# A fused attention, feed-forward and soft-MoE kernel: other column parts at the end, low sums in PSUM, halves before the selector, and a new written order

## The chip, the cores and the metric

The kernel runs on one core of a Trainium2 chip. The time is device microseconds (us) of one launch, measured on the chip; a figure for a kernel is the median of its runs.

## What is computed

Three stages, all in f32 outside (shapes: q, k, v 2 x 8 x 768 x 64; x 1536 x 512; w1 8 x 512 x 1024; w2 8 x 1024 x 512):

```python
# 1. clustered attention, 16 head-batches, 16 centroids per head
q_assign = argmax(einsum('bhsd,hcd->bhsc', q_n, c_n), -1)      # the same for k
scores = where(q_assign == k_assign, q @ k.T / sqrt(D), -1e9)
x = softmax(scores) @ v                                         # -> [1536, 512]
# 2. feed-forward with h * relu6(h + 3) / 6
x = act(x @ w_in) @ w_out                                       # 512 -> 2048 -> 512
# 3. soft MoE: 8 experts with 4 slots each
logits = x @ phi                                                # [1536, 32]
slot_input = softmax(logits, 0).T @ x                           # [32, 512]
slot_out[e] = relu(slot_input[e] @ w1[e]) @ w2[e]
out = softmax(logits, 1) @ slot_out                             # [1536, 512]
```

## The kernel before

The whole program is one function of some 1,170 small generators, most of them a few instructions long between two `yield`s. `ev` (L270) collects them; `flush` (L273) runs them in an order that is written out by hand: the string `ORDER` lists, step by step, the number of the generator that issues its next piece. Each engine works through its instructions in the order in which they were issued, and so does each queue of DMA issues (SP's for loads and half of the stores, ScalarE's for the other half). A second string, `ROOMS`, says which buffer of a pool each named tile gets; a tile's first write waits for the last reader of what stood in that buffer.

**Attention.** A head-batch `i` (called a head below) has queries and keys split into f16 high and low halves and transposed (`qk1t`). `as_mm` (L461) multiplies the twelve 128-row tiles of q and k with the centroids `ct`, which are themselves two f16 halves side by side: a matmul gives 2 x 16 columns, the sums with the centroids' high halves and those with their low halves. ScalarE copies the low columns to a tile `ac`, VectorE adds them to the high ones; then `as_mm` and `as_max` (L486) find the largest of 16 with its index and write a one-hot tile, `as_put` (L504) puts it beside q and k as mask columns, and it is transposed too: for head 0 by TensorE, for the others by a DMA (`qk2t`). `maxq` and `maxr` take the rows' maxima, `shift` (L572) writes them into `qk2t` as one more row, and `scores` (L587) makes the masked scores of which ScalarE takes the exponential. `keep` (L374) issues filler matmuls into a PSUM tile `kw` that nobody reads.

**End.** The slots' input (`slot_in`, `slot_t` L1290) goes through `layer1` (L1409; four experts side by side in 32-column strips, two groups `g`), `relu`, `turn` (transposes) and `layer2` (L1446; group 0) to the slot outputs. Group 1's layer 2 is done in two column parts, `PARTS` (L1017): columns 0 to 383 and then 384 to 511, so that output columns of part 0 leave while part 1 is still computed. `fetch` (L1041) loads the weights over SP's queue, two DMAs of 512 KB for a 1 MB tile `wk_n` (`rooms`, L1023, names the buffer: four of them are the tiles `pr_0` to `pr_3`). The chunks of kind "d" are group 1's second-layer weights `w2[e]`, 1,024 rows as 8 chunks `c` of 128, of which the first half of the tiles (hf 0) takes chunks 1 to 4 of part 0's columns and the whole of chunk 0, the second (hf 1) the rest of part 0, and after all of part 0 the rest of part 1.

`layer2_part` (L1465) computes a part of group 1 and copies it from PSUM to SBUF in f32 (`o2s`). In `o2s` the 32 slots x 4 experts stand as 128 rows of which only each expert's own four slots count. `selectors` (L1340) builds an f32 matrix that picks these rows, three times over; `slots_out` (L1355) multiplies it with `o2s` of both groups (96 rows: three copies of the slots' outputs), ScalarE scales the 96 rows into f16 (`s16`), and VectorE overwrites the last 32 with the rest, the low half. `combine` (L1374) multiplies the combining weights (transposed `cT`) with `s16`, scales, and stores: batch 0 over ScalarE's queue, batch 1 over SP's, in part 0 three stores for each batch, in part 1 one.

## Time and profile before

| | us |
|---|---|
| median of 3 runs (lowest, highest) | 450.44 (450.15, 451.37) |
| the profiled execution: its own time | 451.0 |
| its span | 449.1 |

| engine | busy us | share of the span |
|---|---|---|
| TensorE (PE) | 429.5 | 96% |
| its weight loads (PEld) | 276.1 | 61% |
| ScalarE (ACT) | 309.8 | 69% |
| VectorE (DVE) | 274.9 | 61% |
| GpSimd (POOL) | 251.1 | 56% |

The mean granted clock of TensorE is 0.991 of full speed. The span goes from the first to the last instruction of the profile; the execution's own time is 1.9 us longer. Busy time counts instructions on an engine, not register, semaphore or DMA-issuing ones; the weight loads run beside matmuls. A share of the span is an average over stages of a different kind, so that views by stretch, waits, and the chain of work that ended last are needed beside it.

### The profile page before, as it was taken

The page shows a single profiled execution, that of the slowest core. Times are in us where ns is not written, and L with a number is a line of the kernel's source. Part 1 is how long each engine was busy: PE and PEld are TensorE (multiplying, and loading weights), DVE is VectorE, ACT ScalarE, POOL GpSimd, SP SyncE. Part 2 cuts the span into 40 slices and gives each one's busy share as a digit, 9 for nine tenths or more (in the row PEclk, how much of TensorE's full clock was granted, in tenths as well). Part 3 has the DMA queues.
Part 4 walks back from the last instruction along what each step waited for, and adds up shares of the span by engine and source line. Part 5 has one row for each costly group of instructions (what it writes and reads, how often), then busy time and mean ns, then how long its engine had stood idle before and what let it go on. Part 6 is the DMA issues. An engine that isn't in the chain of part 4 may idle for free.

```text
span 449.1 us, 11732 instructions
## 1 busy us (share of the span) xinstructions
PE 429.5 (96%) x4866; PEld 276.1 (61%) x4866; DVE 274.9 (61%) x479; ACT 309.8 (69%) x508; POOL 251.1 (56%) x229
## 2 busy tenths in 40 slices
PE   8899999999999999999999999999999999889983
PEld 6567778777886556565656567774555445623432
DVE  5989999999866686484666577513434225540322
ACT  7789999988999887888778789874344344501112
POOL 6557588965665676678759788884232333130000
PEclk9999999999999999999999999999999999989997
DMA  8999958997677998407664719907996888799978
GB/s 268 250 201 221 262 89 230 232 234 257 223 173 108 273 260 190 140 14 153 131 165 86 175 22 341 227 14 143 290 393 183 200 216 273 249 378 347 382 211 278
DMA packets 126645, 95.23 MB, mean 212 GB/s; under 512 B 95360, under 2 KB 111744, under 8 KB 126592
## 3 DMA queue, kind: packets, MB, share of 16 engines
q1 hardware_dynamic: 122672, 88.69, 75.1%
q10 hardware_dynamic: 3920, 5.80, 3.6%
q8 instruction: 38, 0.62, 0.6%
q14 instruction: 15, 0.12, 0.1%
HBM read 64.06 MB, written 7.34 MB: 159 GB/s over the span
## 4 chain that ended last, share of the span: by engine, by line
PE 73%; DVE 11%; DMA 6%; ACT 5%; issue 2%; POOL 1%; SPq 0%; DVEq 0%; ACTq 0%; POOLq 0%
PE h L745 27%; PE st L591 5%; PE sm L553 5%; PE st L595 5%; DVE mxs L569 4%; PE acc L661 4%; PE acc L674 3%; DMA wk<-in_moe_w_dram 2%; PE acc L667 2%; PE acc L666 2%; DMA pr<-in_moe_w_dram 2%; PE z L853 2%; PE kw L377 2%; PE lg L796 2%; DMA qk1t<-pr 1%
## 5 line engine op out<-in xcount | busy, mean ns | idle before, releaser
L368 POOL TENSOR_TENSOR pp<-p,pp 128x768 f16<-128x768 f32 x72 | 118.4, 1653 | 46.6 <-ACT pp L358 31.7
L745 PE MATMUL h<-wq,xt 128*128 128x512 f16 x576 | 134.1, 379 | 0.0
L569 DVE TENSOR_REDUCE mxs<-sm 128x1 f32<-128x768 f32 x96 | 89.1, 951 | 20.7 <-PE sm L553 19.9
L745 PEld LDWEIGHTS <-xt 128*128 128x128 f16 x576 | 54.4, 98 | 59.4 <-issue 2.1
L368 POOL TENSOR_TENSOR ghl<-r,ghl 128x1024 f16<-128x1024 f32 (+1 forms) x25 | 50.3, 2014 | 59.1 <-ACT ghl L358 54.6
L639 ACT ACTIVATE p<-st 128x768 f32<-128x768 f32 x72 | 58.2, 811 | 18.3 <-PE st L595 14.4
L358 ACT ACTIVATE pp<-p 128x768 f16<-128x768 f32 x72 | 60.4, 842 | 2.8 <-PE acc L674 1.8
L764 DVE SCALAR_TENSOR_TENSOR r<-r,h 128x1024 f32<-128x1024 f32 (+1 forms) x26 | 29.5, 1137 | 28.6 <-ACT r L762 28.3
L762 ACT ACTIVATE r<-h,b_relu 128x1024 f32<-128x1024 f32 (+1 forms) x26 | 27.1, 1047 | 17.6 <-POOL ghl L368 9.4
L591 PE MATMUL st<-qk1t 128*128 128x384 f16 x144 | 35.1, 325 | 2.3 <-DVE qk2t L578 0.7
L358 ACT ACTIVATE ghl<-r 128x1024 f16<-128x1024 f32 (+1 forms) x26 | 25.5, 986 | 16.1 <-PE z L853 8.4
L667 PE MATMUL acc<-v,pp 128*128 128x64 f16 x432 | 36.1, 194 | 0.0
L666 PE MATMUL acc<-v,pp 128*128 128x65 f16 x432 | 36.1, 192 | 0.0
L661 PE MATMUL acc<-v,pp 128*128 128x65 f32 x288 | 35.6, 273 | 0.0
L661 PEld LDWEIGHTS acc<-v,pp 128*128 128x128 f32 x288 | 34.7, 192 | 0.9
L595 PE MATMUL st<-qk2t 102*128 102x384 f16 x144 | 35.2, 325 | 0.0
L553 PE MATMUL sm<-qk2t 80*128 80x384 f16 x144 | 34.4, 325 | 0.7 <-ACT wot L989 0.2
L666 PEld LDWEIGHTS <-pp 128*128 128x128 f16 x432 | 31.5, 99 | 2.9
L368 POOL TENSOR_TENSOR pr<-pr,pr 128x768 f16<-128x768 f32 x15 | 25.2, 1677 | 13.6 <-ACT pr L358 10.3
L667 PEld LDWEIGHTS <-pp 128*128 128x128 f16 x432 | 29.2, 96 | 2.8
L358 ACT ACTIVATE pr<-pr 128x768 f32<-128x768 f32 (+2 forms) x32 | 26.3, 823 | 4.0 <-DMA qk1t<-pr 2.2
L377 PE MATMUL kw<-ident,ident 128*128 128x256 f16 x136 | 22.9, 294 | 2.6 <-POOL b_relu L870 1.7
(223 smaller groups left out, 801.7 us busy)
## 6 DMA issues: line engine op xcount, KB each, us to landing
wk<-in_moe_w_dram SPq DMA_DIRECT2D x36, 512.0 KB, 6.7
wi<-in_moe_w_in_dram SPq DMA_DIRECT2D x16, 512.0 KB, 6.2
wod<-in_moe_w_out_dram SPq DMA_DIRECT2D x16, 512.0 KB, 4.8
pr<-in_moe_w_dram SPq DMA_DIRECT2D x12, 512.0 KB, 6.5
wos<-wo ACTq DMA_DIRECT2D x8, 512.0 KB, 3.3
wk<-wos SPq DMA_DIRECT2D x8, 512.0 KB, 5.1
pr<-in_q_dram SPq DMA_DIRECT2D x16, 192.0 KB, 4.4
pr<-in_k_dram SPq DMA_DIRECT2D x16, 192.0 KB, 4.3
```

The source lines that it names most:

```text
L358: nc.scalar.activation(out, in_, AF.Copy, scale=scale)
L368: (nc.vector if e == "v" else nc.gpsimd).tensor_tensor(out=out, in0=in_, in1=hi, op=ALU.subtract)
L377: nc.tensor.matmul(t[:, 0, 0:256], ident16, ident.bitcast(F16), start=True, stop=True)
L553: nc.tensor.matmul(s[:, j, 0:384], d["qk2t"][0:80, n, 0], d["qk2t"][0:80, 3 * j : 3 * j + 3, 1], start=True, stop=True,)
L569: nc.vector.tensor_reduce(out=mxs[i % 2][:, 96 + n : 97 + n], in_=s[:, :, 0:384], op=ALU.max, axis=AX.XY)
L591: nc.tensor.matmul(s[:, j, 0:384], d["qk1t"][:, t, 1], d["qk1t"][:, 3 * j : 3 * j + 3, 0], start=True, stop=False)
L595: nc.tensor.matmul(s[:, j, 0:384], d["qk2t"][0 : 96 + NT, t, 1], d["qk2t"][0 : 96 + NT, 3 * j : 3 * j + 3, 0], start=False, stop=True,)
L639: nc.scalar.activation(p32, s[:, :, 0:384], AF.Exp, scale=sc_exp)
L661: nc.tensor.matmul(o, p32[:, j, r * P : (r + 1) * P], d["v32"][:, t], start=(t == 0 and n == 0), stop=False)
L666: nc.tensor.matmul(o, hi, v1[:, t, 0:65], start=(t == 0 and n == 0), stop=False)
L667: nc.tensor.matmul(o[:, 0:64], hi, v1[:, t, 65:129], start=False, stop=False)
L745: nc.tensor.matmul(s[:, fb % 2], xt[:, lhs], wq[fb][:, hl, kk], start=(n == 0), stop=(n == 11))
```

## The change

It has five parts.

1. In `as_mm`, for heads 0 and 1 only, the low centroid sums are added in PSUM: 24 matmuls of 16 columns, two for each tile into the same columns, in place of 12 of 32 columns. The copy by ScalarE and the add by VectorE go.
2. `PARTS` becomes 352 and 160 columns. The loads of the "d" chunks are cut otherwise: for part 0 pairs of chunks (2 x 352 columns, 16 loads, before 8 of 4 or 3 chunks and 4 of chunk 0 whole); then for part 1 four chunks of 160 columns in a load (8 loads, as before).
3. The experts' results go to f16 before the selector: `o2_halves` has ScalarE write the high half, scaled by a mask column that is 2^10 on the group's own rows and 0 elsewhere, and VectorE the low half. The mask is built by VectorE (four reductions of 32 x 2 and a scale). The selector is one f16 matrix for both groups; `slots_out` now issues four f16 matmuls, two for 64 rows (high half, twice) and two for 32 rows (low half), and ScalarE and VectorE each copy their rows to `s16`.
4. `layer2_part` yields after every second chunk, so that its matmuls can be issued in four pieces.
5. `ORDER` and `ROOMS` are new throughout.

```diff
 ORDER = (
-    "0 837 807 9 811 8 9 809 0 15 15 803 829 840 0 0 0 16 16 16 16 16 5 10 8 11 13 13 842 848 834 820 8 8 16 16 8 "
+    "9 9 8 15 13 15 16 16 0 13 0 0 1131 840 838 810 822 808 832 7 828 8 12 16 16 8 842 16 818 11 16 16 8 827 8 836 "
...
@@ -463,21 +463,29 @@
         d = st[i]
         pm = psm(f"as_{i}")
         a2 = pm[:, 0 : 24 * C].rearrange("p (n l c) -> p n l c", l=2, c=C)
+        a = a2[:, :, 0]
         for n in range(2 * NT):
-            nc.tensor.matmul(
-                a2[:, n],
-                d["qk1t"][:, n // 2, n % 2],
-                ct[:, :, h * C : (h + 1) * C],
-                start=(n == 0),
-                stop=(n == 2 * NT - 1),
-            )
-        yield
-        a = a2[:, :, 0]
-        ac = sm.tile([P, 12, C], F32, tag="ac", name=f"ac_{i}", bufs=1)
-        nc.scalar.copy(ac, a2[:, :, 1])
-        yield
-        nc.vector.tensor_tensor(out=a, in0=a, in1=ac, op=ALU.add)
-        yield
+            x = d["qk1t"][:, n // 2, n % 2]
+            if i < 2:
+                for l in range(2):
+                    nc.tensor.matmul(
+                        a[:, n],
+                        x,
+                        ct[:, l, h * C : (h + 1) * C],
+                        start=(n == 0 and l == 0),
+                        stop=(n == 2 * NT - 1 and l == 1),
+                    )
+            else:
+                nc.tensor.matmul(
+                    a2[:, n], x, ct[:, :, h * C : (h + 1) * C], start=(n == 0), stop=(n == 2 * NT - 1)
+                )
+        yield
+        if i >= 2:
+            ac = sm.tile([P, 12, C], F32, tag="ac", name=f"ac_{i}", bufs=1)
+            nc.scalar.copy(ac, a2[:, :, 1])
+            yield
+            nc.vector.tensor_tensor(out=a, in0=a, in1=ac, op=ALU.add)
+            yield
         mx = sm.tile([P, 12], F32, tag="mx", name=f"mx_{i}", bufs=2)
         nc.vector.tensor_reduce(out=mx, in_=a, op=ALU.max, axis=AX.X)
         nc.vector.tensor_tensor(out=a, in0=a, in1=mx.unsqueeze(2).to_broadcast([P, 12, C]), op=ALU.is_equal)
@@ -1014,7 +1022,7 @@
 
 
     NG = E // 4
-    PARTS = [(0, 384), (384, 128)]
+    PARTS = [(0, 352), (352, 160)]
     chunks = [("o", c, 0) for c in range(4)]
     chunks += [("1", 4 * g + j, hf) for g in range(NG) for hf in range(2) for j in range(4)]
     chunks += [("2", 4 * g + j, hf) for g in range(NG - 1) for hf in range(2) for j in range(4)]
@@ -1042,40 +1050,22 @@
         n = ring["n"]
         ring["n"] += 1
         kind, e, hf = chunks[n]
-        if kind == "d" and hf == 1:
-
+        if kind == "d":
             ts = []
-            for j in range(4):
+            for j in range(4 if hf else 1):
                 t = room(n + j, rooms[n + j], 2048, f"wk_{n + j}")
-                u = t[:, 0:1152].rearrange("p (c d) -> p c d", c=3)
-                v = t[:, 1152:2048].rearrange("p (c d) -> p c d", c=7)
-                for c in range(1, 8):
-                    wd[e + j, 1, c] = v[:, c - 1]
-                for c in range(5, 8):
-                    wd[e + j, 0, c] = u[:, c - 5]
-                ts.append((u, v))
-            for j in range(4):
+                for p, (c0, w) in enumerate(PARTS):
+                    u = wd[e + j, p, hf] = t[:, 4 * c0 : 4 * c0 + 4 * w].rearrange("p (c d) -> p c d", c=4)
+                    for c in range(4):
+                        wd[e + j, p, 4 * hf + c, "w"] = u[:, c]
+            todo = [(0, hf, r, 2, j) for r in (0, 2) for j in range(4 if hf else 1)]
+            if hf:
+                todo += [(1, f, 0, 4, j) for f in range(2) for j in range(4)]
+            for p, f, r, m, j in todo:
+                c0, w = PARTS[p]
                 src = w2[e + j].rearrange("(p c) d -> p c d", c=8)
-                nc.sync.dma_start(ts[j][0], src[:, 5:8, 0:384])
+                nc.sync.dma_start(wd[e + j, p, f][:, r : r + m], src[:, 4 * f + r : 4 * f + r + m, c0 : c0 + w])
                 yield
-            for lo, hi in ((1, 4), (4, 8)):
-                for j in range(4):
-                    src = w2[e + j].rearrange("(p c) d -> p c d", c=8)
-                    nc.sync.dma_start(ts[j][1][:, lo - 1 : hi - 1], src[:, lo:hi, 384:512])
-                    yield
-            return
-        if kind == "d":
-            src = w2[e].rearrange("(p c) d -> p c d", c=8)
-            t = room(n, rooms[n], 2048, f"wk_{n}")
-            u = t[:, 512:2048].rearrange("p (c d) -> p c d", c=4)
-            wd[e, 0, 0] = t[:, 0:384]
-            wd[e, 1, 0] = t[:, 384:512]
-            for c in range(1, 5):
-                wd[e, 0, c] = u[:, c - 1]
-            nc.sync.dma_start(u, src[:, 1:5, 0:384])
-            yield
-            nc.sync.dma_start(t[:, 0:512], src[:, 0])
-            yield
             return
         if kind == "1":
             src = w1[e].rearrange("(p k) f -> p k f", k=4)[:, 2 * hf : 2 * hf + 2]
@@ -1338,38 +1328,42 @@
         nc.vector.tensor_copy(cT, tp)
 
     def selectors():
-        sel = sl["sel"] = lt2k("a1", 0, [NG, 3, NS], F32)
-        nc.gpsimd.memset(sel, 0.0)
-        yield
-        for g in range(NG):
-            for j in range(4):
-                for i3 in range(3):
-                    c0 = 16 * g + 4 * j
-                    nc.gpsimd.tensor_copy(
-                        sel[32 * j : 32 * j + 32, g, i3, c0 : c0 + 4],
-                        ident[32 * j : 32 * j + 32, 32 * j + c0 : 32 * j + c0 + 4],
-                    )
-            yield
-
+        sel = sl["sel"] = lt2k("a1", 0, [3, NS], F16)
+        nc.gpsimd.tensor_copy(sel, i4.unsqueeze(1).to_broadcast([P, 3, NS]))
+        yield
+        m = sl["mask"] = sm.tile([P, NG], F32, tag="mx2", name="mask", bufs=2)
+        for j in range(4):
+            b = ident[32 * j : 32 * j + 32, 32 * j : 32 * j + 32].rearrange("p (g j i) -> p g j i", g=NG, j=4)
+            nc.vector.tensor_reduce(out=m[32 * j : 32 * j + 32], in_=b[:, :, j], op=ALU.add, axis=AX.X)
+        yield
+        nc.vector.tensor_scalar(out=m, in0=m, scalar1=SO, scalar2=None, op0=ALU.mult)
+
+    def o2_halves(g, c0, w, src):
+        if ("o2s", g) not in sl:
+            sl["o2s", g] = lt2k("w1", g, [2, 512], F16)
+        hi, lo = (sl["o2s", g][:, a, c0 : c0 + w] for a in range(2))
+        m = sl["mask"][:, g : g + 1]
+        nc.scalar.activation(hi, src, AF.Identity, scale=m)
+        yield
+        nc.vector.scalar_tensor_tensor(out=lo, in0=src, scalar=m, in1=hi, op0=ALU.mult, op1=ALU.subtract)
 
     def slots_out(p):
         c0, w = PARTS[p]
         so = sl["so", p] = psm(f"so_{p}")
-        for g in range(NG):
-            nc.tensor.matmul(
-                so[0:96, 0:w],
-                sl["sel"][:, g].rearrange("p a s -> p (a s)"),
-                sl["o2s", g][:, c0 : c0 + w],
-                start=(g == 0),
-                stop=(g == NG - 1),
-            )
-        yield
+        sel = sl["sel"].rearrange("p a s -> p (a s)")
         s16 = sl["s16", p] = lt2k("a1", 1 + p, [512], F16)[:, 0:w]
-        nc.scalar.activation(s16[0:96], so[0:96, 0:w], AF.Copy, scale=SO)
-        yield
-        nc.vector.scalar_tensor_tensor(
-            out=s16[64:96], in0=so[64:96, 0:w], scalar=SO, in1=s16[64:96], op0=ALU.mult, op1=ALU.subtract
-        )
+        for a, (r0, r1) in enumerate(((0, 64), (64, 96))):
+            for g in range(NG):
+                nc.tensor.matmul(
+                    so[r0:r1, 0:w],
+                    sel[:, r0:r1],
+                    sl["o2s", g][:, a, c0 : c0 + w],
+                    start=(g == 0),
+                    stop=(g == NG - 1),
+                )
+                yield
+            (nc.vector.tensor_copy if a else nc.scalar.copy)(s16[r0:r1], so[r0:r1, 0:w])
+            yield
 
     def combine(p, b):
         c0, w = PARTS[p]
@@ -1458,9 +1452,7 @@
         yield
 
     def store2(g):
-        sl["o2s", g] = lt2k("w1", g, [512], F32)
-        nc.vector.tensor_copy(sl["o2s", g], sl["o2", g])
-        yield
+        yield from o2_halves(g, 0, 512, sl["o2", g])
 
     def layer2_part(p, i):
         c0, w = PARTS[p]
@@ -1471,15 +1463,14 @@
                 nc.tensor.matmul(
                     sl["o2", NG - 1, p][32 * j : 32 * j + 32, 0:w],
                     hw(NG - 1, c, j),
-                    wd[E - 4 + j, p, c],
+                    wd[E - 4 + j, p, c, "w"],
                     start=(c == 0),
                     stop=(c == 7),
                 )
-        yield
+            if c % 2:
+                yield
         if i:
-            if p == 0:
-                sl["o2s", NG - 1] = lt2k("w1", NG - 1, [512], F32)
-            nc.vector.tensor_copy(sl["o2s", NG - 1][:, c0 : c0 + w], sl["o2", NG - 1, p][:, 0:w])
+            yield from o2_halves(NG - 1, c0, w, sl["o2", NG - 1, p][:, 0:w])
 
     for n in range(14):
         ev(keep, 47 + n, 2)
```

Besides what is shown below, two things of the new order bear on what follows. The fillers: head 0's assignment stands behind six filler matmuls after the transposed centroids, before four; and six stand between the slots' input (`si`, L1281) and the matmuls that transpose it (`sit`, L1298), where none stood. Up to the last scores of head 0 there are 90 fillers (before 98), between those and the last scores of all 16 (before 14), and in the whole program as many as before (136). And SP issues the transposition of head 2's `qk2` tile ahead of the two 512 KB loads of the weight `wi_1_0`, before it stood behind them.

VectorE at the start, head 0's assignment (`as`: the centroid sums; `ac`: the copied low sums; `mx`: the maxima; `ohs`: the one-hot tile). Before:

```order
L419 COPY pr_3_106<-tq1_1_191 128x6x128
L896 COPY ct_94<-ctp_233 128x256
L479 TENSOR_TENSOR as_0_250<-as_0_250,ac_0_270 128x12x16
L482 TENSOR_REDUCE mx_0_283<-as_0_250 128x12
L483 TENSOR_TENSOR as_0_250<-as_0_250,mx_0_283 128x12x16
L491 TENSOR_TENSOR as_0_250<-as_0_250,rank_90 128x12x16
L494 TENSOR_REDUCE mx2_0_287<-as_0_250 128x12
```

In the changed kernel:

```order
L419 COPY pr_3_106<-tq1_1_215 128x6x128
L904 COPY ct_94<-ctp_229 128x256
L490 TENSOR_REDUCE mx_0_292<-as_0_251 128x12
L491 TENSOR_TENSOR as_0_251<-as_0_251,mx_0_292 128x12x16
L499 TENSOR_TENSOR as_0_251<-as_0_251,rank_90 128x12x16
L502 TENSOR_REDUCE mx2_0_296<-as_0_251 128x12
```

The add of `ac` is gone, and the reduction follows the copy of the centroids.

SP near the end, the last second-layer weights of group 0 (`wk_2x`, `pr_0`, `pr_1`) and the first "d" chunks (`pr_2`, `pr_3`, `wk_3x`). Before:

```order
L1097 DMA wk_23_6731<-in_moe2_w2_dram 128x1024 x2
L1097 DMA wk_24_6734<-in_moe2_w2_dram 128x1024 x2
L1097 DMA wk_25_6737<-in_moe2_w2_dram 128x1024 x2
L1097 DMA pr_0_103<-in_moe2_w2_dram 128x1024
L1097 DMA pr_1_104<-in_moe2_w2_dram 128x1024
L1075 DMA pr_2_105<-in_moe2_w2_dram 128x4x384
L1075 DMA pr_3_106<-in_moe2_w2_dram 128x4x384
L1075 DMA wk_30_6763<-in_moe2_w2_dram 128x4x384
L1077 DMA wk_30_6763<-in_moe2_w2_dram 128x512
L1097 DMA pr_1_104<-in_moe2_w2_dram 128x1024
L1077 DMA pr_3_106<-in_moe2_w2_dram 128x512
```

In the changed kernel:

```order
L1087 DMA wk_24_6762<-in_moe2_w2_dram 128x1024 x2
L1087 DMA wk_25_6765<-in_moe2_w2_dram 128x1024
L1087 DMA pr_0_103<-in_moe2_w2_dram 128x1024
L1087 DMA pr_1_104<-in_moe2_w2_dram 128x1024
L1087 DMA wk_25_6765<-in_moe2_w2_dram 128x1024
L1067 DMA pr_2_105<-in_moe2_w2_dram 128x2x352
L1087 DMA pr_0_103<-in_moe2_w2_dram 128x1024
L1067 DMA pr_3_106<-in_moe2_w2_dram 128x2x352
L1067 DMA pr_2_105<-in_moe2_w2_dram 128x2x352
L1087 DMA pr_1_104<-in_moe2_w2_dram 128x1024
L1067 DMA wk_30_6776<-in_moe2_w2_dram 128x2x352
L1067 DMA wk_31_6778<-in_moe2_w2_dram 128x2x352 x2
```

The second half of `wk_25` now stands behind the first halves for `pr_0` and `pr_1`, and the loads of the "d" chunks are in smaller pieces.

VectorE at the end, from layer 2's part 0 on (`o2_1_p`: group 1's sums of part p; `so_p`: the selected rows; `po_p_b_u`: the combined output of part p, batch b). Before:

```order
L1482 COPY late_w1_6846<-o2_1_0_6865 128x384
L1370 SCALAR_TENSOR_TENSOR late_a1_6699<-so_0_6899,late_a1_6699 32x384
L1399 TENSOR_SCALAR late_w2_6922<-po_0_0_1_6927 128x768
L1399 TENSOR_SCALAR late_w3_6936<-po_0_1_0_6937 128x768
L1482 COPY late_w1_6846<-o2_1_1_6904 128x128
L1370 SCALAR_TENSOR_TENSOR late_a1_6699<-so_1_6968,late_a1_6699 32x128
L1399 TENSOR_SCALAR late_b0_6746<-po_1_1_0_6976 128x384
L1399 TENSOR_SCALAR late_w1_6846<-po_1_0_1_6992 128x384
L1399 TENSOR_SCALAR late_gt_6923<-po_0_1_2_6961 128x768
```

In the changed kernel:

```order
L1348 SCALAR_TENSOR_TENSOR late_w1_6835<-o2_1_0_6860,mask_6828,late_w1_6835 128x352
L1365 CAST late_a1_6629<-so_0_6900 32x352
L1393 TENSOR_SCALAR late_w2_6907<-po_0_0_1_6912 128x704
L1393 TENSOR_SCALAR late_w3_6931<-po_0_1_0_6932 128x704
L1348 SCALAR_TENSOR_TENSOR late_w1_6835<-o2_1_1_6922,mask_6828,late_w1_6835 128x160
L1393 TENSOR_SCALAR late_gt_6908<-po_0_1_2_6948 128x704
L1365 CAST late_a1_6629<-so_1_6975 32x160
L1393 TENSOR_SCALAR late_b0_6721<-po_1_1_0_6982 128x480
L1393 TENSOR_SCALAR late_w1_6835<-po_1_0_1_6999 128x480
```

The copy of `o2_1_0` has become the low half's instruction (ScalarE's high half goes ahead of it), the low half behind the selector has become a copy to f16, and the low half of part 1 has moved ahead of the last scaling of part 0.

## Rows read from the trace of the kernel before

**Rows 1.** Page, part 1: busy time, share of the span and instructions.

```profile
PE 429.5 (96%) x4866; PEld 276.1 (61%) x4866; DVE 274.9 (61%) x479; ACT 309.8 (69%) x508; POOL 251.1 (56%) x229
```

**Rows 2.** Stretches: from:to, length, busy us by engine, PEclk, DMA share, GB/s.

```profile
37.00:50.00 13.00, 12.47 (x163) 9.74 (x163) 12.50 (x22) 12.72 (x20) 9.14 (x6) 1.00 0.96 260
300.00:350.00 50.00, 50.00 (x455) 26.86 (x452) 19.91 (x34) 21.45 (x44) 19.54 (x11) 1.00 0.77 227
...
25.00:375.00 350.00, 346.56 (x4010) 1.00 0.76 189
```

(Engines in the first two rows: PE, PEld, DVE, ACT, POOL; in the third PE alone.)

**Rows 3.** TensorE's waits: line, waited for, total us, times, longest us.

```profile
PE st L591 <- DVE qk2t L578: 0.7, 1, 0.7
PE as L467 <- DMA qk1t<-pr: 0.6, 1, 0.6
...
PE sit L1298 <- DVE late_x L1292: 0.9, 1, 0.9
```

**Rows 4.** The chain that ended last: start us, us, what.

```profile
18.55 6.28 DMA qk1t<-pr
...
399.61 1.64 PE e L1414 x8
...
405.80 0.86 PE e1b L1414 x8
...
419.49 11.06 DMA wk<-in_moe_w_dram
...
430.59 2.12 PE o L1471 x18
432.71 1.61 PE so L1359 x4
...
434.35 0.50 ACT late_a L1368
...
434.87 0.57 DVE late_a L1370
...
435.48 0.50 PE po L1393 x2
...
437.82 1.01 PE o L1471 x32
```

**Rows 5.** Stretches of the end, columns as in rows 2 (all engines).

```profile
400.00:404.00 4.00, 4.00 (x28) 1.10 (x24) 3.14 (x9) 0.52 (x1) 0.00 (x0) 0.58 0.97 375
404.00:408.00 4.00, 4.00 (x44) 1.20 (x40) 0.02 (x1) 0.00 (x0) 0.00 (x0) 1.00 0.91 294
420.00:424.00 4.00, 4.00 (x47) 1.61 (x44) 0.96 (x1) 0.00 (x0) 0.00 (x0) 1.00 1.06 376
434.00:438.00 4.00, 3.60 (x53) 2.03 (x55) 2.13 (x3) 1.45 (x3) 0.00 (x0) 1.00 0.23 68
438.00:447.20 9.20, 3.78 (x60) 2.85 (x50) 2.85 (x6) 2.50 (x5) 0.00 (x0) 0.84 1.00 334
```

**Rows 6.** Timeline of 8 to 9.7 us: start us, us, engine, line, what.

```profile
8.22 0.45 PE L467 MATMUL as<-ct,pr 128*128 128x32 f16 x12
...
8.52 1.36 PE L377 MATMUL kw<-ident,ident 128*128 128x256 f16 x11
8.70 0.32 ACT L477 COPY ac<-as 128x192 f32<-128x192 f32 x1 [0.85 <-PE as L467]
...
9.06 0.37 DVE L479 TENSOR_TENSOR as<-as,ac 128x192 f32<-128x192 f32 x1 [0.89 <-ACT ac L477]
9.46 0.36 DVE L482 TENSOR_REDUCE mx<-as 128x12 f32<-128x192 f32 x1
```

**Rows 7.** Timeline of the end, columns as in rows 6.

```profile
432.75 0.56 DVE L1482 COPY late_w<-o 128x384 f32<-128x384 f32 x1 [6.60 <-PE o L1471]
...
436.84 0.91 ACTq L1404 DMA_DIRECT2D out_dram<-late_w  x2
...
442.70 0.55 SPq L1404 DMA_DIRECT2D out_dram<-late_gt  x1
```

326 rows, old and new, of tables (ORDER, ROOMS) are left out of this document.

## The prediction, made before the result was seen

> **What bounds the kernel now.** I read the page's busy times first [rows 1]: TensorE is busy for 96% of the span, no other engine for over 69%. That is a mean over stages, so the next view is the busy time of each engine by stretch [rows 2]. From 37 to 50 us VectorE and ScalarE are busy for 12.50 and 12.72 of 13 us; from 300 to 350 us TensorE is busy for all 50 us and the others for half of that or less. Between 25 and 375 us it is busy for 346.56 of 350 us, and the longest of its waits there are 0.7 and 0.6 us [rows 3]: 3.4 us of holes in all, so the middle is a column of matmuls. The chain of waits that ended last [rows 4] shows another regime near the end: it stands in DMA from before 419.49 us, for 11.06 us in one piece, until the last weights of layer 2's first part land at 430.55 us. The stretches of the end [rows 5] say why: the DMA engines are full by 420 us (share 1.06, 376 GB/s in 420 to 424 us), nearly idle from 434 to 438 us (0.23) and full again from 438 to 447.2 us (1.00), when the output leaves. So there are three stages: a start on VectorE and ScalarE, a middle on TensorE, an end on DMA with one hole in it.
>
> **The change part by part.**
>
> *Low centroid sums in PSUM (heads 0 and 1).* Now twelve matmuls start at 8.22 us and the filler behind them at 8.52 us [rows 6], 25 ns each; then ScalarE copies (0.32 us), VectorE adds (0.37 us), and the reduction starts at 9.46 us: 1.24 us from first matmul to reduction. With 24 matmuls I add 12 x 25 ns = 0.30 us (below: 0.15, the columns are halved; above: 0.45, the whole group's row again). The reduction can start after 0.45 + 0.30 + 0.04 us of handing over, 0.79 us, so 0.45 us are saved. The order puts six fillers instead of four between the transposed centroids and these matmuls; at the 0.12 us of a filler (1.36 us for eleven [rows 6]) that takes 0.25 us back. For head 1 VectorE loses one more add of 0.37 us in a stretch in which it hardly rests [rows 2]. Sum for VectorE's shift of head 0, which lets the first scores start: 0.45 - 0.25 + 0.37 = 0.57 us earlier. Behind it TensorE now waits 0.6 us for head 2's transposed tile [rows 3], whose DMA took 6.28 us [rows 4] behind 1 MB of the first weight; SP now issues that transpose ahead of that megabyte, so I let nothing take the place of the 0.57 us. **Start: -0.6 us**, between 0 (the fillers eat it) and -1.2 us (0.57 and the 0.6 us wait).
>
> *New sequence in the middle.* It holds the same matmuls, and 14 fillers before and 16 now, so its TensorE work is the same. What it can win is the 3.4 us of waits, and not all of it, since VectorE and ScalarE are as full as before; what it can lose has no row and is the first rival. **Middle: 0**, within 1 us either way.
>
> *Widths 352 and 160.* Before, layer 2's first part could end once 8 x 384 columns of four experts had landed, and with them chunk 0's other 128: 4 x 128 x 3,200 x 4 bytes = 6.55 MB. Now it is 4 x 128 x 2,816 x 4 = 5.77 MB, 0.79 MB less; at 376 GB/s [rows 5] that is 2.1 us earlier. The pieces come in pairs of chunks, so behind the last one five matmuls (10 rows) are left where 18 rows took 2.12 us [rows 4]: 2.12 x 10/18 x 352/384 = 1.08 us, 1.0 us less.
>
> *Expert results halved first.* Now the way from the last matmul (432.71 us) to the combining matmuls (435.48 us) takes 2.77 us [rows 4]: a copy of 0.56 us [rows 7] under two f32 selector matmuls, then ScalarE 0.50 and VectorE 0.57 us. The new way is ScalarE's scaled half (128x352; nearest row 96x384, 0.50: 0.46), VectorE's low half (nearest 0.57: 0.52), the two selector matmuls that still wait (nearest the combining pair, 0.50: 0.46; below, one pair as fast as it is streamed, 0.2), VectorE's cast (at most 0.52) and four handings over of 0.04: 2.1 us. Saved 0.7 us, between 0.4 and 1.0. The mask's five small VectorE instructions fall at a time when VectorE waits for layer 2, and cost nothing; without that cover about 1 us.
>
> Together the first store, now at 436.84 us [rows 7], would be issued 2.1 + 1.0 + 0.7 = 3.8 us earlier, at 433.0 us. But the end waits for DMA: all loads and stores have the same bytes in sum, so what can be won is the hole, 4 x 0.77 = 3.1 us [rows 5]. Part 0's six stores (2.16 MB at the 334 GB/s of that stage: 6.5 us) then follow the loads until about 441 us. Part 1 is what is late next: 160 columns make its last loads, matmuls (now 1.01 us [rows 4], 1.27) and chain longer, about 3.8 us from its last landing near 436 us to its first store, so 439.8 us if nothing holds up the loads. If the stores that start at 433.0 us hold them up for their remaining 1.5 us, it is 441.3, and data a microsecond later; I take half of that hole, 0.5 us. In SP's order the second half of one 1 MB weight tile moves behind two loads that wait for layer 1 to free their rooms; there the DMA share is 0.91 now [rows 5], and a 512 KB piece is 1.3 us, so it costs between 0 and 0.9 us; I take 0.3. **End: -3.1 + 0.5 + 0.3 = -2.3 us**, between -3.1 and -0.5.
>
> The rule that bears on that 0.5 us is in the Trainium skill, "DMA: Bandwidth & Descriptors", section "Queues, rings and completion order": each DMA engine goes round between the queues it has work for. By that rule the stores of ScalarE's queue take turns with the loads of SP's, and the loads left would take twice their time; no stretch of this trace has loads and stores at once. The sum by it is the third rival's.
>
> **Sum.** -0.6 + 0 - 2.3 = -2.9 us. The profiled execution took 451.0 us (span 449.1 and 1.9 around it), which gives 448.1; the median of the runs, 450.44, lies 0.56 lower, so 447.5 us.
>
> **Rivals.** *Slower: the middle.* Between 12 and 150 us the new order lets a head's shift on VectorE come later than TensorE needs it. For it: VectorE and ScalarE have no reserve there [rows 2], and one such wait exists (scores on the shift, 0.7 us [rows 3]). Against: the order of a head's steps is nearly the same in both. Its price is 0.7 us for each head; it decides from the fifth of the first eight heads on, and with all eight it is 5.6 us: 453.1 us.
>
> *More: the clock.* From 400 to 404 us TensorE's granted clock is 0.58 [rows 5], that is, it falls to its lower level of 1.2 GHz after TensorE had stood idle 0.9 us before the slots' transposing matmuls [rows 3], and layer 1's first eight rows take 1.64 us where later ones take 0.86 [rows 4]. Six fillers now stand in that hole. If the clock stays up, layer 1 ends up to 1.9 us earlier and frees the rooms of the waiting loads; the DMA can use 0.3 us of my cost and the new hole's 0.5, and the 0.5 us that the shares of 0.97 and 0.91 leave in 400 to 408 us [rows 5], 1.3 us in all: 446.2 us.
>
> *Same: the end gives it back.* Loads and stores that take turns put part 1's last landing at 437.5 us or later, its two larger stores are alone at the end, and the start's gain drowns in the fillers. Left are 0.9 us: 449.5 us. That part 0's edit does nothing, because its copy and add were not on the path, is inside this case.
>
> **How the numbers follow.** The measurement tells a change of about 0.3%, 1.35 us, from none. The forecast gets 0.46 (own range 446.2 to 448.9), the clock 0.22, the end given back 0.20, the middle 0.12. Faster takes the first two, 0.68; same 0.20; slower 0.12. The range goes from -1.2 - 1 - 3.1 = 445.1 us to no gain at the start, 1 us lost in the middle and 0.5 won at the end, 450.9 us; beyond it lie most of the slow rival and little else.
>
> **What would show it.** Right: the reduction of head 0 near 9.2 us after the first matmul ran at about 8.4; first store near 433 us; DMA share near 1 from 420 us to the end, no stretch like 434 to 438; the last store issued before 441 us. Wrong: TensorE waits in the middle that sum to well over 3.4 us; a DMA hole between the stores of part 0 and part 1; a first store near 433 us with an end that hardly moved. A granted clock of 1.00 from 400 to 404 us is the second rival.

## The result, and the profile after

The changed kernel is slower: 455.25 us (median of 6 runs, 453.44 to 456.56) against 450.06 us (6 runs, 448.75 to 451.37). The ratio is 1.0116, with a 95% interval of 1.0086 to 1.0147. The forecast was 447.5 us, in a range that ended at 450.9. The profiled execution took 456.51 us, with a span of 454.6 us (before 449.1). Two kernels of the experiments below had runs that took some per cent longer at a lower mean clock, and their ratios leave these out: one of the seven runs of a1_swap (458.09 us) and two of the four of b1_swap (461.10 and 462.59 us).

The page, part 1, of the changed kernel [rows 1 before]:

```profile
PE 433.9 (95%) x4890; PEld 279.9 (62%) x4890; DVE 274.2 (60%) x482; ACT 310.2 (68%) x509; POOL 247.5 (54%) x205
```

TensorE is busy 4.4 us longer with 24 matmuls more, which at the 25 ns of [rows 6] are 0.6 us. The rest must be matmuls that ran slower; the clock further down shows which. Landmarks of the two profiled executions show where the time went; the third column belongs to the experiment `a3_early` below.

| us | before | after | a3_early |
|---|---|---|---|
| head 0's first scores | 25.2 | 23.8 | 24.5 |
| head 1's first scores | 38.0 | 44.1 | 37.0 |
| last matmul that moves x into the slots (`z`) | 388.1 | 393.3 | 386.4 |
| layer 1's first matmul | 399.61 | 404.79 | 397.80 |
| first store issued | 436.84 | 440.54 | 432.75 |
| last load landed | 436.57 | 443.18 | 435.53 |
| last store issued | 442.70 | 448.56 | 440.91 |
| end of the span | 449.1 | 454.6 | 446.9 |

Head 0 is 1.4 us earlier, head 1 is 6.1 us later, and layer 1 starts 5.2 us late; the end of the span is 5.5 us late. What was lost was lost between head 0's and head 1's scores. TensorE's waits in the changed kernel (line, waited for, total us, times, longest us) name one that [rows 3] did not have:

```profile
PE sm L561 <- DMA qk2t<-pr: 4.0, 1, 4.0
PE so L1357 <- ACT late_a L1365: 1.1, 2, 0.6
PE si L1271 <- DVE late_x L1258: 0.9, 1, 0.9
```

For 4.0 us TensorE stands before the matmuls `sm` from which head 1's maxima are taken, and waits for head 1's second transposed tile `qk2t`. SP's timeline of the changed kernel (start us, us, queue, line, what) shows what stood ahead of that transposition:

```profile
19.80 1.45 SPq L443 DMA_TRANSPOSE qk1t<-pr  x1
21.29 1.35 SPq L938 DMA_DIRECT2D wi<-in_moe_w_in_dram  x2
22.74 2.01 SPq L523 DMA_TRANSPOSE qk2t<-pr  x1
```

and the same view of the kernel before:

```profile
15.21 0.91 SPq L930 DMA_DIRECT2D wi<-in_moe_w_in_dram  x2
18.55 2.17 SPq L443 DMA_TRANSPOSE qk1t<-pr  x1
22.83 1.43 SPq L515 DMA_TRANSPOSE qk2t<-pr  x1
```

`wi` is the tile `wi_1_0`, two loads of 512 KB; the `qk1t` is head 2's (the section on the change calls it head 2's `qk2` tile, wrongly), the `qk2t` is head 1's. Before, the megabyte was issued 3.3 us ahead of the first of the two transpositions. Now it stands between them. The second is issued at the same time as before, 22.74 against 22.83 us. The chain of waits of the changed kernel (start us, us, what) shows how long it then took, and what followed:

```profile
22.74 9.00 DMA qk2t<-pr
31.79 2.10 PE sm L561 x6
...
404.79 1.06 PE e L1408 x8
...
436.68 0.56 ACT late_w L1346
437.28 0.32 PE so L1357
437.63 0.45 ACT late_a L1365
...
438.68 0.53 DVE late_a L1365
439.25 1.06 PE po L1387 x6
```

It took 9.00 us, before 3.87 (22.83 to 26.70). The second load of the megabyte, issued ahead of it at 22.20 us, lands at 28.30 us, and the transposition 3.4 us after that: most of the 9.00 us is the time until the megabyte is down. The stretches of the changed kernel (columns as in [rows 2]: PE, PEld, DVE, ACT, POOL, granted clock, DMA share, GB/s) show a second loss behind the first:

```profile
27.70:31.80 4.10, 0.12 (x5) 0.02 (x2) 1.47 (x4) 2.52 (x5) 0.75 (x1) 0.94 1.18 143
31.80:41.50 9.70, 9.70 (x62) 7.02 (x63) 5.87 (x8) 3.81 (x5) 2.53 (x2) 0.50 0.93 264
41.50:45.00 3.50, 3.50 (x43) 2.98 (x43) 3.36 (x5) 3.46 (x5) 2.65 (x2) 1.00 0.00 0
...
404.00:408.00 4.00, 3.62 (x36) 1.36 (x39) 2.25 (x7) 0.00 (x0) 0.00 (x0) 1.00 1.03 421
...
436.00:440.00 4.00, 2.42 (x16) 0.90 (x10) 1.11 (x2) 1.25 (x3) 0.00 (x0) 1.00 1.06 296
440.00:444.00 4.00, 4.00 (x71) 2.21 (x69) 1.78 (x2) 1.26 (x2) 0.00 (x0) 1.00 0.91 302
444.00:448.00 4.00, 2.64 (x31) 1.88 (x24) 2.34 (x5) 2.02 (x5) 0.00 (x0) 0.96 0.77 279
```

After TensorE has stood idle, its granted clock is 0.50, the lower level of 1.2 GHz, for 9.7 us in which it is busy without a break; then it is 1.00 again. At the lower level a pair of 128x384 matmuls takes 0.84 us, later 0.48. Half of 9.7 us is 4.9 us of lost work at most; a2_fill below measures about 4.0 us up to head 1's scores. Wait and clock so make about 8 us, less the 1.4 us of the earlier start 6.6; head 1's scores are 6.1 us late.

### The profile page after: what moved, and what is told of

It reads as the page before. It is cut to its first block, busy times and chain, and to the rows that moved or that the text cites. A ratio compares the mean times of both kernels' runs of the same rounds, so it can differ in the third digit from the quotient of the medians.

```text
span 454.6 us, 11756 instructions
## 1 busy us (share of the span) xinstructions
PE 433.9 (95%) x4890; PEld 279.9 (62%) x4890; DVE 274.2 (60%) x482; ACT 310.2 (68%) x509; POOL 247.5 (54%) x205
## 4 chain that ended last, share of the span: by engine, by line
PE 75%; DMA 9%; DVE 8%; ACT 3%; issue 1%; POOL 1%; SPq 0%; DVEq 0%; ACTq 0%
PE h L753 28%; PE sm L561 6%; PE st L599 5%; PE st L603 5%; PE acc L669 4%; DMA wk<-in_moe_w_dram 4%; DVE mxs L577 3%; PE acc L675 3%; PE acc L674 3%; PE acc L682 2%; DMA qk2t<-pr 2%; DMA qk1t<-pr 2%; PE z L861 2%; PE lg L804 2%; PE e L1408 2%; PE e1b L1408 1%
## 5 line engine op out<-in xcount | busy, mean ns | idle before, releaser
L577 DVE TENSOR_REDUCE mxs<-sm 128x1 f32<-128x768 f32 x96 | 89.4, 953 | 25.2 <-PE sm L561 24.5
L561 PE MATMUL sm<-qk2t 80*128 80x384 f16 x144 | 36.1, 341 | 4.5 <-DMA qk2t<-pr 4.0
L669 PEld LDWEIGHTS acc<-v,pp 128*128 128x128 f32 x288 | 36.3, 199 | 1.1 <-issue 0.2
L669 PE MATMUL acc<-v,pp 128*128 128x65 f32 x288 | 36.8, 279 | 0.0
L368 POOL TENSOR_TENSOR pr<-pr,pr 128x768 f16<-128x768 f32 x15 | 24.7, 1647 | 15.7 <-ACT pr L358 15.6
```

The source lines that it names most:

```text
L368: (nc.vector if e == "v" else nc.gpsimd).tensor_tensor(out=out, in0=in_, in1=hi, op=ALU.subtract)
L561: nc.tensor.matmul(s[:, j, 0:384], d["qk2t"][0:80, n, 0], d["qk2t"][0:80, 3 * j : 3 * j + 3, 1], start=True, stop=True,)
L577: nc.vector.tensor_reduce(out=mxs[i % 2][:, 96 + n : 97 + n], in_=s[:, :, 0:384], op=ALU.max, axis=AX.XY)
L669: nc.tensor.matmul(o, p32[:, j, r * P : (r + 1) * P], d["v32"][:, t], start=(t == 0 and n == 0), stop=False)
```

## The experiments

My theory was that the place of the megabyte in SP's queue is the whole loss. The rivals were the idle clock alone (the hole should be filled, not closed), the narrower loads of the end, and the three code edits by themselves. In the edits below, numbers are steps of `ORDER`: 854 issues the loads of `wi_1_0`, 855 its conversion, 67 head 1's `as_put` with its transposition. All ratios are to the kernel before as it ran in the same rounds, with 95% intervals; its median there was 449.05 us (a1_swap, a2_fill, b1_swap, a5_parts), 449.73 us (a3_early, a6_late, b5_all, b2_halves) and 449.21 us (the others).

**a1_swap: the megabyte behind head 1's transposition.** SP's order against the changed kernel:

```diff
 DMA_TRANSPOSE qk1t_2
-DMA wi_1_0 x2
 DMA_TRANSPOSE qk2t_1
+DMA wi_1_0 x2
```

> The changed kernel with one step moved: the two 512 KB loads of wi_1_0 go to SP's queue behind the transposition of head 1's qk2 tile, not ahead of it. Nothing is left out. Theory A (the megabyte ahead of that transposition makes it land 5.0 us later, 31.74 in place of 26.70 us, TensorE waits 4.0 us for it, and what it issues afterwards runs at a granted clock of half until about 40.7 us): the wait of 4.0 us is gone, the transposition lands at 27 to 28 us, the granted clock of 25 to 50 us is 1.00 in place of 0.80, head 1's first scores start near 37 us (before 38.0, changed 44.1), and the time is 448 to 450 us. Theory B (the new order of the middle is slower by itself, VectorE being full there, and the wait only shows it): the time stays at 453 us or more, and another wait or a late maximum on VectorE takes the place of the 4.0 us.

Measured: 453.86 us (all seven runs), 1.0082 (1.0054 to 1.0109). The 4.0 us wait of TensorE is gone, but most of the loss is not. The waits from 25 to 50 us of this kernel say why:

```profile
DVE pr L918 <- DMA wi<-in_moe_w_in_dram: 4.0, 1, 4.0
PE acc L667 <- DVE ohs L502: 2.8, 1, 2.8
```

Now VectorE stands 4.0 us at the first conversion of `wi_1_0`, which lands at 30.68 us. Behind it on VectorE are head 2's one-hot tile and head 1's maxima. TensorE then waits 2.8 us for that one-hot tile, and its granted clock from 25 to 50 us is 0.86. The wait has moved from one engine to another.

**a2_fill: the changed kernel's order with the hole filled.** 34 filler matmuls more; their step, which held two, is moved to stand behind head 1's counts:

```diff
 def keep(n, m):
-    for _ in range(m):
+    for _ in range(36 if n == 39 else m):
```

> The changed kernel with 36 filler matmuls in the hole (34 more than now, at 0.108 us each 3.9 us), behind head 0's counts and ahead of head 1's first maxima; SP's order is as in the changed kernel, so the transposition lands as late. Nothing is left out. Theory A1 (of the 7 us lost between 25 and 45 us, 4.0 are the wait and the rest is the half clock that follows the idle time): the granted clock of 25 to 50 us is 1.00, head 1's first scores start 2 to 3.5 us earlier than 44.1 us, and the time is 452 to 453.5 us. Theory A2 (the lost clock costs nothing, since VectorE's six maxima of 0.97 us for each head set the pace behind the late transposition): the clock is 1.00 and the time stays within 0.7 us of 455.3 us.

Measured: 454.02 us, 1.0089 (1.0060 to 1.0118). The stretch from 25 to 50 us of this kernel:

```profile
25.00:50.00 25.00, 24.65 (x281) 19.40 (x279) 19.61 (x37) 20.51 (x32) 15.78 (x13) 1.00 0.94 212
```

The clock stays at 1.00 (the changed kernel has 0.80 there). Head 1's scores come 3.1 us and the last `z` matmul 2.65 us earlier than in the changed kernel, though head 0's are 0.9 us later (24.7 us): from head 0's scores to head 1's it takes 16.3 us, in the changed kernel 20.3. So the clock's part of the loss is real, about 4.0 us of the 4.9 that it could be. The spans differ by only 1.7 us, since the way from layer 1 to the end is a microsecond longer here (50.7 against 49.8 us): the last load lands 39.4 us after layer 1's first matmul, there 38.4; why, no view settled. The medians differ by 1.2 us, and their intervals overlap, so a gain in the whole time is not shown.

**b1_swap: the kernel before with the megabyte moved.** Nothing else of the change is in it:

```diff
-DMA wi_1_0 x2
 DMA_TRANSPOSE qk1t_2
 DMA pr_0 (q)
+DMA wi_1_0 x2
 DMA_TRANSPOSE qk2t_1
```

> The kernel before with one step moved the other way: the two 512 KB loads of wi_1_0 go behind the transposition of head 2's qk1 tile and ahead of that of head 1's qk2 tile, as the changed kernel has it. Nothing else of the change is in it, nothing is left out. Theory A: that transposition lands near 31 us, TensorE waits 3 to 4 us for it, the granted clock falls behind it, and the time is 454 to 458 us. Theory B (the late transposition only matters with the new order): 450 to 452 us.

Measured: 453.91 (the profiled execution) and 456.34 us, 1.0124 (1.0084 to 1.0165), from these two runs. This one move makes the kernel before about as slow as the changed one. TensorE's waits and the stretch of this kernel:

```profile
PE sm L550 <- DMA qk2t<-pr: 2.2, 1, 2.2
```

```profile
25.00:50.00 25.00, 22.81 (x236) 16.72 (x232) 19.70 (x37) 19.61 (x32) 13.40 (x8) 0.86 0.86 191
```

The same wait and a lowered clock, both smaller than in the changed kernel. Head 1's scores come at 43.2 us (before 38.0), and layer 1 starts 5.1 us later than before. The cause is sufficient by itself.

**a5_parts: a1_swap with the old widths.**

```diff
-    PARTS = [(0, 352), (352, 160)]
+    PARTS = [(0, 384), (384, 128)]
```

> As the first run of these (wi_1_0 behind the transposition), with the parts of 384 and 128 columns again; the loads stay cut in pairs of chunks, and the halves before the selector stay. Nothing is left out. Theory of the forecast (part 0's loads end 0.79 MB / 376 GB/s = 2.1 us earlier with 352 columns, and this fills the hole before the stores): this run is 1 to 2.5 us slower than the first of these, its first store goes out 1.5 to 2.5 us later. Rival (what is won at part 0 is given back by part 1, whose wider columns are late next, so the width does not matter): within 0.5 us of the first run. Rival of the other sign (part 1 with 160 columns sets the end): 0.5 to 2 us faster.

Measured: 453.96 us, 1.0087 (1.0062 to 1.0111), the same as a1_swap within what these runs can tell. The widths are neither the loss nor a gain that shows.

**a3_early: the megabyte ahead of both transpositions, as before the change.**

```diff
+DMA wi_1_0 x2
 DMA_TRANSPOSE qk1t_2
-DMA wi_1_0 x2
 DMA_TRANSPOSE qk2t_1
```

> The changed kernel with one step moved: the two 512 KB loads of wi_1_0 go to SP's queue ahead of the transposition of head 2's qk1 tile, where the kernel before has them. Nothing is left out. Theory A, restated after the first four runs (both places behind that transposition are too late: ahead of head 1's qk2 tile the loads delay the transposition, 4.0 us of wait on TensorE, and behind it they land at 30.7 us while VectorE stands 4.0 us before the first conversion of wi_1_0, with head 2's one-hot and head 1's maxima queued behind it): neither wait is there, wi_1_0 lands before 24 us, TensorE waits at most 1 us for head 2's qk1 tile, the granted clock of 25 to 50 us is 1.00, head 1's first scores start at 37 to 39 us, and the time is 448 to 451 us. Theory B (the new order loses its time elsewhere too): the clock is 1.00 and the time stays at 452 us or more.

Measured: 449.09 us, 0.9989 (0.9971 to 1.0007). The loss of 1.16% is gone whole, and the rest of the change comes out as no difference. SP's timeline of this kernel has the old order, and times within 1.0 us of the old ones:

```profile
16.23 0.90 SPq L936 DMA_DIRECT2D wi<-in_moe_w_in_dram  x2
19.45 2.28 SPq L441 DMA_TRANSPOSE qk1t<-pr  x1
21.82 1.54 SPq L521 DMA_TRANSPOSE qk2t<-pr  x1
```

Its stretches at the start and the end:

```profile
25.00:50.00 25.00, 24.49 (x289) 19.35 (x288) 23.62 (x42) 24.16 (x38) 19.67 (x15) 1.00 0.87 213
...
432.00:436.00 4.00, 3.87 (x60) 1.99 (x62) 1.78 (x2) 1.48 (x2) 0.00 (x0) 1.00 0.99 317
436.00:440.00 4.00, 2.64 (x41) 1.95 (x31) 2.16 (x4) 1.67 (x4) 0.00 (x0) 1.00 0.77 275
440.00:444.00 4.00, 1.45 (x14) 1.05 (x12) 0.66 (x1) 0.56 (x2) 0.00 (x0) 1.00 0.85 276
```

**a6_late: a1_swap with the conversion of `wi_1_0` behind head 1's maxima on VectorE.** One step 855 moves behind the last of head 1's `maxr`:

```diff
-TENSOR_SCALAR pr_1<-wi_1_0
 TENSOR_REDUCE mx_2
 TENSOR_TENSOR ohs
 ...
+TENSOR_SCALAR pr_1<-wi_1_0
 TENSOR_REDUCE mxs (head 1, last)
```

> The changed kernel with the loads of wi_1_0 behind the transposition of head 1's qk2 tile, and the first conversion of wi_1_0 on VectorE moved behind head 1's maxima and its second part with it. Nothing is left out. Theory A: no engine waits for these loads any more, VectorE's idle time of 4.0 us before the conversion is gone, the granted clock of 25 to 50 us is 1.00, head 1's first scores start at 37 to 39 us, 448 to 451 us. Theory B: the time stays at 452 us or more. If the conversion is late next, VectorE's work between 35 and 60 us is pushed together and 1 to 2 us of the gain are given back.

Measured: 450.82 us, 1.0023 (1.0005 to 1.0041). With VectorE freed, 0.59 of the 0.82% that a1_swap lost come back. About a quarter stays. The views can't say much about it, since the profiled execution was the slowest of the ten (453.52 us): in it the clock from 25 to 50 us is still 0.86, and head 1's scores come at 40.0 us (a3_early 37.0). The loads of head 4's q and k, which stand behind the megabyte, land late in their turn; whether they are what is left, no run tells apart.

**b2_halves, b5_all, b4_as, b3_parts: the code edits on the old order.** b2 is the expert results in halves alone, b4 the low sums in PSUM alone, b3 the widths and their loads alone, b5 all three. In b2_halves and b5_all the mask's scaling stands behind group 0's halves, so that group 0's expert results lack their factor of 2^10; the instructions are the same. The diffs are those of the section on the change: part 3, part 1, part 2, and these three together. Part 4, the yields, is in none of them.

> The kernel before with one edit alone: expert results are masked, scaled and cut into f16 halves first and then moved by the f16 selector; the parts stay at 384 and 128 columns. Nothing is left out. Forecast of the step: the way from layer 2's last matmul of part 0 to the combining matmuls takes 2.1 us where it took 2.77, the first store goes out 0.4 to 1.0 us earlier, and the time is 0.3 to 1.0 us shorter if the idle DMA engines before the first store are the bound. Rival (part 1 sets the end): the first store is earlier and the time the same within 0.3 us. If the four matmuls and two copies in a row take longer than the two f32 matmuls, 0.3 to 1 us slower.

> The kernel before, its order and its rooms, with the three edits of the code alone: low centroid sums in PSUM for heads 0 and 1, parts of 352 and 160 columns with their loads, and halves before the selector; steps that have become more pieces issue them where the old step stood. Nothing is left out. Theory of the forecast (the edits win at the start and at the end what was worked out, and the loss is the new order's): 2 to 3.5 us faster than the kernel before, 446 to 447.5 us. Rival (the end is bound by loads and stores whose bytes are the same, so only the start's half microsecond is left): 0 to 1 us faster. Rival of the other sign (part 1's 160 columns end later than the old 128): 0.5 to 2 us slower.

> The kernel before, its order and its rooms, with one edit alone: the low centroid sums of heads 0 and 1 are added in PSUM. Nothing is left out. Forecast of the step without the two more fillers of the new order: head 0's reduction starts 0.45 us earlier, head 0's and head 1's shift 0.45 to 0.8 us earlier, and the time is 0.3 to 0.8 us shorter, unless TensorE's wait for head 2's transposed tile takes it back: then head 1's scores start as before and the time is the same within 0.3 us.

> The kernel before, its order and its rooms, with one edit alone: parts of 352 and 160 columns, and the changed kernel's loads for them (pairs of chunks, 16 loads of 352 KB for part 0). Nothing is left out. Forecast of the step (part 0's loads end 2.1 us earlier, its matmuls 1.0 us after that): 1 to 3 us faster than before. Theory D, from the run of all three edits with the old order (3 us slower; part 0's last load landed 31.1 us after layer 1's first matmul, before 30.9, though 0.79 MB fewer were to land): SP stands at a wait for a free room with only two loads of 352 KB in flight where two of 768 KB were, so the DMA engines run dry between 408 and 416 us; then this run is 2 to 4 us slower than the kernel before, and the DMA share of 408 to 416 us is below 0.9 (before 1.03 and 1.05). Theory E (the slower run came from the other two edits): within 1 us of the kernel before.

Measured: halves 449.29 us, 0.9988 (0.9973 to 1.0002); widths 450.40 us, 1.0025 (1.0006 to 1.0044); low sums 450.89 us, 1.0038 (1.0015 to 1.0061); all three 452.79 us, 1.0074 (1.0048 to 1.0101). a3_early, in the same rounds, has these three edits on the new order, with the yields, at 0.9989: there the order and the yields together make up for what the edits cost on the old order, 0.85%. No part of the change gives a gain that can be measured on the old order, against forecasts of 0.3 to 3.5 us for each, and two cost a little. For the widths, the stretches before layer 2 show a DMA that moves less, here b3_parts:

```profile
408.00:412.00 4.00, 4.00 (x44) 1.26 (x40) 0.19 (x1) 0.60 (x1) 0.00 (x0) 1.00 0.98 339
412.00:416.00 4.00, 4.00 (x42) 2.04 (x38) 1.88 (x3) 1.77 (x3) 0.00 (x0) 1.00 0.97 352
```

where the kernel before has shares of 1.03 and 1.05, and b5_all 0.90 and 0.87. On the new order the same pieces don't show it: a3_early has 1.05 and 1.06. For the low sums, VectorE's and GpSimd's timelines of b4_as and of the kernel before differ in one place. b4_as:

```profile
10.61 0.36 DVE L501 TENSOR_TENSOR ohs<-as,mx 128x192 f16<-128x192 f32 x1
10.88 1.80 DVE L917 TENSOR_SCALAR pr<-wi 128x1024 uint32<-128x1024 uint32 x1
13.93 0.55 DVE L416 COPY pr<-tq 128x768 f16<-128x768 f16 x1
```

```profile
10.52 0.92 POOL L365 TENSOR_TENSOR v<-v,v 128x384 f16<-128x384 f32 x1
```

The kernel before:

```profile
11.39 0.68 DVE L912 TENSOR_SCALAR pr<-wi 128x1024 uint32<-128x1024 uint32 x1
...
13.32 0.55 DVE L419 COPY pr<-tq 128x768 f16<-128x768 f16 x1
```

```profile
11.45 1.40 POOL L368 TENSOR_TENSOR v<-v,v 128x384 f16<-128x384 f32 x1
```

The one-hot tile is 0.5 us earlier (10.61 against 11.11 us), and that brings the weight's conversion to a time at which GpSimd's instruction is already running. It takes 1.80 us in place of 0.68, the copy behind it starts 0.6 us later than before, and TensorE waits 1.0 us for VectorE's conversion ahead of head 0's maxima, where it did not wait before (line, waited for, total us, times, longest us):

```profile
PE kw L374 <- DVE wi L921: 1.0, 1, 1.0
```

Head 0's scores come at 25.3 us, as before (25.2). That is why the 0.5 us win nothing; why the median of b4_as is 1.7 us above the kernel before, with runs from 448.9 to 453.6 us, stays open.

**b7_wide: b3_parts with whole pieces of four chunks.**

```diff
-todo = [(0, hf, r, 2, j) for r in (0, 2) for j in range(4 if hf else 1)]
+todo = [(0, hf, 0, 4, j) for j in range(4 if hf else 1)]
```

> As the run with the parts of 352 and 160 columns alone, but part 0's loads take four chunks at once (8 loads of 704 KB in place of 16 of 352 KB), so that twice the bytes are in flight at each wait of SP. Nothing is left out. Theory D: the DMA share of 408 to 416 us is back above 0.95, part 0's last load lands 1.5 to 3 us earlier than with pairs, and the time is 1.5 to 4 us shorter than there. Theory E: no difference to the run with pairs beyond 0.7 us.

Measured: 449.17 us, 0.9996 (0.9981 to 1.0011). The same stretches of this kernel:

```profile
408.00:412.00 4.00, 4.00 (x40) 1.08 (x36) 0.00 (x0) 0.07 (x1) 0.00 (x0) 1.00 1.06 374
412.00:416.00 4.00, 4.00 (x40) 1.95 (x32) 1.72 (x3) 1.71 (x3) 0.00 (x0) 1.00 1.04 394
```

The DMA is full again, and the widths' 0.25% are back. The two differ by 1.2 us in their medians, and their intervals overlap only between 1.0006 and 1.0011. That the size of the pieces did it is likely, but the traces don't settle it: part 0's last load lands about equally late in both (427.4 us, in b3_parts 427.8), while layer 1 ran at a granted clock of 0.73 from 400 to 404 us here and of 1.00 in b3_parts.

**c1_evac: a3_early with the last scalings and stores of part 0 ahead of part 1's halves.** On VectorE, and likewise on ScalarE:

```diff
+TENSOR_SCALAR late_gt<-po_0_1_2 128x704
 SCALAR_TENSOR_TENSOR late_w1<-o2_1_1,mask,late_w1 128x160
-TENSOR_SCALAR late_gt<-po_0_1_2 128x704
```

> The changed kernel with the loads of wi_1_0 in their old place, and one more step moved: the scaling and stores of part 0's last two thirds of batch 1 (ScalarE and VectorE, 0.76 and 0.89 us) are issued ahead of part 1's halves, not behind them. Nothing is left out. Theory F (at the end these two stand in the queues of ScalarE and VectorE behind halves that wait for part 1's last matmul, so their stores go out at 438 us though their sums are ready at 434 us, and the DMA share of 436 to 440 us is 0.77): their stores are issued 2 to 2.5 us earlier, ScalarE is free for part 1's copy, the last store goes out 0.2 to 0.5 us earlier and lands 0.7 to 1.5 us earlier, and the time is 0.7 to 1.5 us shorter than the 449.1 us of the run with wi_1_0 moved alone. Rival (part 1's chain of 5.4 us from its last load to its last store sets the end): within 0.5 us of that run.

Measured: 449.06 us, 1.0003 (0.9982 to 1.0023). Part 0's last store for batch 1 is issued at 436.41 us, in a3_early at 438.52, yet the last store of all is issued at 440.55, in a3_early at 440.91. The stretches of this kernel:

```profile
432.00:436.00 4.00, 4.00 (x58) 2.08 (x62) 1.74 (x3) 1.51 (x2) 0.00 (x0) 0.74 1.00 335
436.00:440.00 4.00, 2.82 (x42) 2.13 (x35) 1.92 (x5) 1.50 (x4) 0.00 (x0) 1.00 0.77 275
440.00:444.00 4.00, 1.10 (x11) 0.74 (x8) 0.48 (x1) 0.21 (x1) 0.00 (x0) 1.00 0.71 222
```

The hole has moved from part 0's stores to the time before part 1's. No gain shows in the time, which fits the rival: part 1's chain sets the end, that is its last weights, its matmuls, and the steps from them to the last store. This one execution is not a clean comparison, though: its last load lands at 434.50 us, 1.0 us earlier than in a3_early, and its granted clock is 0.74 from 432 to 436 us (a3_early 1.00), so that part 1's matmuls start later than its loads allow.

No version of these is shown to be faster than the kernel before. a3_early undoes the change's loss: its ratio of 0.9989 against 1.0116 is 1.27%, 5.7 us.

## Why the prediction was wrong

**The step that failed** is in the start: "SP now issues that transpose ahead of that megabyte, so I let nothing take the place of the 0.57 us." I followed head 2's transposition, which the megabyte had been ahead of, and did not ask which transposition the megabyte was now ahead of. It was head 1's second one, which TensorE needs first. The term of -0.6 us became 4.0 us of waiting and about 4.0 us by the clock, less 1.4 us by which head 0 was earlier: about +6.6 us by this sum, and 6.1 us measured at head 1's scores, where -0.6 stood. a3_early and b1_swap show it from both sides: one move takes the loss out of the new kernel, and the like move puts it into the old one.

**The slow rival** gave 453.1 us, nearer to the truth than the forecast, but by another mechanism: scores that wait 0.7 us for VectorE's shift in each of eight heads. The trace has one wait of 4.0 us on a DMA. So a slower kernel was among the cases, but not for this reason.

**Low sums.** Reduction after the first matmul: 0.79 us predicted, 0.79 measured (8.32 to 9.11 us). Its use was over-sized: alone on the old order it brings nothing, since the conversion behind it collides with GpSimd. The row is 1.80 us in place of 0.68 for VectorE in one kernel, and 1.40 in place of 0.92 for GpSimd in the other, whichever started second. The Trainium skill, "SBUF — State Buffer", section "SBUF: two separate sides", says that VectorE and GpSimd share a pair of ports which the first to start holds for its whole instruction, where VectorE's instruction is of a kind that uses this pair. Here the trace agrees in direction in both kernels.

**Middle.** Predicted 0 within 1 us. In a3_early, which has the new order without the misplaced megabyte, head 0's scores are 0.7 us earlier than before and the last `z` matmul 1.7: the middle gave 1.0 us (the same in c1_evac), the edge of the range. Right.

**Halves.** The way from part 0's last matmul to the combining matmuls was to fall from 2.77 to 2.1 us. It measures 436.64 to 439.25, 2.6 us, and in b2_halves, with the old 384 columns, 431.18 to 434.02, 2.8 us: the halves saved nothing there, and the 0.15 us here go with the narrower columns. What the sum did not have is in the waits above: the two selector matmuls for the low half wait for ScalarE's copy of the high rows, 0.6 us at the longest. By the handings over alone I had let them run beside it.

**Widths and the end.** In a3_early the first store comes 34.95 us after layer 1's first matmul, before 37.23: 2.3 us of the 3.8 predicted. Part 0's last load gave 1.3 of these (29.6 us after layer 1's first matmul, before 30.9; 2.1 predicted), the matmuls behind it 0.75 (1.0 predicted), the halves 0.15 (0.7 predicted). The hole before that store is gone (share 0.99 in 432 to 436 us, before 0.23 in 434 to 438 [rows 5]). But the end takes 49.1 us from layer 1's first matmul, before 49.5: 0.4 us won of 2.3. The rest went into the last load, which lands 37.7 us after layer 1's first matmul (before 37.0), into a new hole before part 1's stores, 4 x (0.23 + 0.15) = 1.5 us in 436 to 444 us, where I had allowed 0.5, and into the finish: in a3_early the last store lands 1.8 us before the span ends, in the kernel before 0.9. From the last landing to part 1's first store it takes 4.6 us (435.53 to 440.13), where the sum had 3.8. So the end's term of -2.3 us was over-sized too. The outcome is that of the third rival, "the end gives it back", but its mechanism, loads and stores that take turns, is not shown (below). As a sum it would have given no measurable gain even without the megabyte, which is what a3_early measures.

**Stores against loads.** I had allowed 0.5 us for the last loads being held up by the first stores. In a3_early the first store is issued at 432.75 us, and the last loads land at 432.63, 433.61, 434.58 and 435.53 us. They are 1.0 us apart before and after the first store, so the hole in front of part 1 is not a delay of the loads by the stores. The Trainium skill, "DMA: Bandwidth & Descriptors", section "Queues, rings and completion order", says that each DMA engine goes round between the queues it has work for; the doubling of the loads' time that I took from this is not seen in these rows. They are no test of it either: from 433.5 to 435.5 us ScalarE's queue, which has the stores, moved 0.56 MB and SP's 0.10 MB, so that nearly all of the loads' bytes had moved before the stores came.

**The clock rival** was right as a row; its price is not settled. Layer 1 starts at 404.79 us in the changed kernel, and from 404 to 408 us the granted clock is 1.00 (before, from 400 to 404 us, 0.58 [rows 5]); layer 1 takes 13.9 us in place of 15.6. The six fillers are not needed for that in every execution: the profiled ones of b2_halves and b3_parts, on the old order, have 1.00 from 400 to 404 us too. In b2_halves, whose loads are cut as before, the last load lands 35.7 us after layer 1's first matmul, before 37.0. These 1.2 us between two executions are near the rival's 1.3; on the new order the end shows no such gain, and no run tells what took it.

One caution on sums: the profiled executions alone would make a3_early 2.2 us faster than the kernel before (446.9 against 449.1 us of span). The profiled execution of before took 451.0 us against a median of 450.06, that of a3_early 448.85 against 449.09. Most of the difference lies in which execution was profiled.

## What to carry to other kernels

When a large load moves past one transfer in a queue, list every transfer that now stands behind it, and ask of each when its reader wants it; the one that was helped is not the one to price. A wait that starves TensorE costs twice here, once as the wait and once as the lower clock after it. Before crediting a faster early stage, ask what comes last behind it: here 2.3 us of earlier stores ended as 0.4 us.
